# Softmax weights and q in one PSUM bank, output banks seeded by ScalarE, a half chunk in two matmuls, gate sums on GpSimd and ScalarE

## The chip, the core and the metric

The kernel runs on one core of a Trainium2 chip. The metric is the device time of one execution in microseconds, less being better. Engines are named as the profile names them: PE is TensorE (PEld its weight loads), DVE is VectorE, ACT is ScalarE, POOL is GpSimd, and SP is the queue that issues most transfers.

## The reference

For x of 2048 tokens by 640, a sliding, dilated attention (32 heads of 20, a window of 8 tokens at distance 2) is mixed by a gate per token with an MLP (640 to 1728 to 640, Mish):

```python
qkv = (x @ wqkv).reshape(B, S, 3, H, Dh)              # H = 32, Dh = 20
idx = pos[:, None] - 2 * arange(8)[None, :]           # idx < 0 is masked
logits = where(mask, einsum("bhsd,bhswd->bhsw", q, kg) * Dh ** -0.5, -1e9)
a = einsum("bhsw,bhswd->bhsd", softmax(logits), vg).reshape(B, S, D) @ wo
h = einsum("bsd,df->bsf", x, w1) + b1
b = einsum("bsf,fd->bsd", h * tanh(softplus(h)), w2)
g = sigmoid((x * gate_w).sum(-1, keepdims=True))
return g * a + (1 - g) * b
```

All data is float32.

## The kernel before

Every matrix product is made from split numbers: an operand X is kept as a high half (X rounded to fp32r, written by ScalarE) and a low half (X minus the high half, written by VectorE or GpSimd), both in one `pair` buffer, and `mm3` runs three matmuls: high by high, high by low, low by high. A matmul has up to 512 columns and adds into one PSUM bank of 128 x 512 floats.

The stages, in the order of TensorE's work: `qkv` makes q, k and v in eight units u (four groups of eight heads, two halves P of the tokens), each of eight banks with 496 columns; ScalarE empties these banks (`qkv_evac`). Between the units runs `mlp1`, the first MLP product, one bank of 15 matmuls per row chunk and token block, whose results (Mish on ScalarE) are stored, and partly summed with accumulating transfers issued by GpSimd (`plus`). Then `mlp2`, the second MLP product: it uses a scheme with seven block products (a, b, c, e, g, d, f in this order; `PRODUCTS`) in place of eight, over seven chunks kc of 128 rows; the seventh chunk of the second half of the 1728 rows has 64 real rows, and the rest is filled. Results of one product in a bank are copied out, and later products add on in the same bank, or VectorE adds the parts. Last, `wo_out` multiplies the attention's output by wo for each of four token blocks tb, and VectorE adds the gated MLP rows (L954) into the buffer that is sent out.

The attention itself (`attention`) runs on VectorE beside TensorE's work, in half units of four slots: `scores` multiplies q with a window of k (L424) and sums over the head's 20 elements (L427), `bounded` adds the mask to the first token's row on GpSimd (L435), `softmax` and `shares` make weights (L452, into `pw`), and `outputs` multiplies them with a window of v (L458) and adds up the window (L463 to L466). `turned_out` stores the result to `o`. `gate_dots` makes the gate sums on VectorE (L582).

The order of the work on each engine is set once, at build time, by `Plan.run`: a planner plays all tasks through with an estimated duration each, and gives every engine the ready task with the lowest rank. A task of engine "ANY" (most low halves) goes to GpSimd when one may run there, and to VectorE when it is due: its first matmul is less than NEAR nanoseconds of TensorE work away. While large attention tasks are left, GpSimd may start such tasks only in the stretches named quiet. Buffers come from rings (`bank`, `pair`, `raw`, `hb`, `w`), and a task that takes one waits for it.

Of the kernel before, what the change touches and what calls it, by code (L numbers as in the profile page):

```python
# [58 lines left out]
class Plan:  # L59


    NEAR, PATIENCE = 8000, 2000
# [31 lines left out]
    def run(self):  # L94
# [6 lines left out]
        loud = sum(t.kind != "" for t in self.tasks)  # L101
# [16 lines left out]
        def due(t):  # L118
            return now - t.rdy > self.PATIENCE if t.need is None else t.need - begun_pe < self.NEAR
# [9 lines left out]
        while left:  # L129
            again = not events or events[0][0] > now  # L130
            while again:
                again = False
                for e in self.LAG:
# [26 lines left out]
                    if e == "POOL" and on and quiet > now and gate and ins:  # L160
                        self.follow(ins, gate)
                    if e == "DVE":
                        if t.kind:
# [21 lines left out]
            if what == "idle":  # L185
                busy[x] = False
                continue
# [25 lines left out]
def kernel(ctx: ExitStack, tc: tile.TileContext, x, wq, wo, w1, b1, w2, xt, gw, out):  # L213
# [6 lines left out]
    psum = ctx.enter_context(tc.tile_pool(name="psum", bufs=8, space=PSUM))  # L220
# [8 lines left out]
    plan = Plan({"bank": 8, "pair": NPAIR, "w": NW, "raw": NRAW, "raw1": 1, "hb": NH,  # L229
                 "ot": 1, "b": 11}, follow)  # L230

    def ps_buf():
        return plan.buf("bank", lambda: psum.tile([128, 512], F32, name="bank"))
# [46 lines left out]
    bound = keep.tile([1, 7, 7], F32)  # L280
# [24 lines left out]
    pw = at.tile([128, 8, W, HQ], F32, name="pw")  # L305
# [18 lines left out]
    def consts_g():  # L324
        for i in range(2):
            G.memset(KV[i][0:1, 0:7], 0.0)

        G.memset(bound, 0.0)
        G.affine_select(bound, bound, pattern=[[1, 7], [1, 7]], compare_op=OP.is_ge,
                        fill=-BIG / scale, base=-7, channel_multiplier=0)  # L330
# [68 lines left out]
    freed = {}  # L399
    spilled = {}  # L400
# [3 lines left out]
    def attention(u, P, hq, ready, gates):  # L404
# [17 lines left out]
        def scores(s0, rank, after):  # L422
            def mul():
                return V.tensor_tensor(pr, window(kv, s0, 0), q[:, s0:s0 + 2, None, :].to_broadcast([128, 2, W, QF]), op=OP.mult)  # L424

            def red():
                V.tensor_reduce(lg_w[:, s0:s0 + 2], pr.rearrange("p s w (h d) -> p s w h d", d=DH), op=OP.add, axis=AX.X)  # L427

            step = chain(rank)
            step("DVE", 2850, mul, ready[s0] + after, kind="qk")  # L430
            return step("DVE", 2750, red, kind="qk sum")

        def bounded(a, b, after):
            b = min(b, 7)
            return add("POOL", 3400, lambda: G.tensor_tensor(lg[0:1, a:b, :, 0:7], lg[0:1, a:b, :, 0:7],  # L435
                       bound[:, a:b, None, :].to_broadcast([1, b - a, HQ, 7]), op=OP.add), [cg] + after, rank=-1)
# [9 lines left out]
        def shares(a, rank, after):  # L446
# [4 lines left out]
            step("DVE", 230, lambda: V.tensor_tensor(sm[:, h], sm[:, h], gate[:, P, h, None].to_broadcast([128, 4, HQ]), op=OP.mult), gates)  # L451
            return step("DVE", 650, lambda: V.tensor_tensor(pw[:, h].rearrange("p s w h -> p s h w"), lg[:, h], sm[:, h, :, None].to_broadcast([128, 4, HQ, W]), op=OP.mult))  # L452

        def outputs(s0, rank, after):
            def mul():
                vw = window(kv, s0, 1)
                vw = bass.AP(tensor=vw.tensor, offset=vw.offset, ap=[list(d) for d in vw.ap[:3]] + [[DH, HQ], [1, DH]])
                V.tensor_tensor(pr.rearrange("p s w (h d) -> p s w h d", d=DH), vw,  # L458
                                pw[:, s0:s0 + 2, :, :, None].to_broadcast([128, 2, W, HQ, DH]), op=OP.mult)

            step = chain(rank)
            step("DVE", 2850, mul, after, kind="pv")
# [15 lines left out]
        for i, a in enumerate((4, 0)):  # L478
            h = 2 * u + i
            read, used = shared_out.get(h - 2, (None, None))  # L480
            t1 = scores(a + 2, turn_of(h - 1, 0), [read, prev])
            t2 = scores(a, turn_of(h - 1, 3), [t1])
            e = softmax(a, turn_of(h - 1, 6), [bounded(a, a + 4, [t1, t2])])
            w = shares(a, turn_of(h, 1), [e, used])
# [588 lines left out]
```

## Time and profile before

| | |
|---|---|
| time, median of 3 runs | 639.48 us (639.43 to 639.97) |
| profiled execution | span 636.9 us from first to last instruction; the page gives no other time for it |
| TensorE | 631.9 us busy, 2805 matmuls, granted clock 1.00 |
| VectorE | 584.1 us busy, 584 instructions |
| ScalarE | 277.4 us busy, 565 instructions |
| GpSimd | 215.2 us busy, 157 instructions |
| transfers | 137 MB, 216 GB/s in the mean |

A row of the profile names the line of the kernel, the engine, the operation, the buffer written and those read, the count, the busy time and mean duration in ns of one instruction, and after the second bar the idle time ahead of them with what ended it. A row of the timeline begins with its start and its duration in us. Line numbers of before and of the changed kernel differ: in the changed one `mm3` is L410 to L412, the splits are L375 and L378, and the output copies are L1063.

### The profile page before, as it was taken

The numbers are of one execution on the slowest core, as the hardware profiler recorded it, in microseconds if no ns is written. First come the engines' busy times: TensorE is split into PE (matmuls) and PEld (weight loads), VectorE is DVE, ScalarE is ACT, GpSimd is POOL, SyncE is SP. The second block draws the span as 40 slices with busy tenths as digits, with TensorE's granted clock in tenths as the row PEclk, the third lists the DMA queues.
The fourth block names the chain that finished last, engine by engine and source line by source line (L and its number), as shares of the span: only waits on it lengthen the run. The fifth ranks groups of instructions, "written<-read, shape, count | busy, mean of one in ns | idle before, by whom it ended". The sixth has DMA issues, their size and how long they took to land.

```text
span 636.9 us, 8494 instructions
## 1 busy us (share of the span) xinstructions
PE 631.9 (99%) x2805; PEld 526.2 (83%) x2805; DVE 584.1 (92%) x584; ACT 277.4 (44%) x565; POOL 215.2 (34%) x157
## 2 busy tenths in 40 slices
PE   9999999999999999999999999999999999999997
PEld 6888888888888888888888888888888888888886
DVE  7888999999999999999899989799999999999941
ACT  7553353435436332542524244584676426721100
POOL 2212313131414442132343423204107328967310
PEclk9999999999999999999999999999999999999999
DMA  9999998867954994798499955989996758844642
GB/s 327 373 283 180 190 263 227 229 174 223 296 172 86 271 258 93 222 218 178 84 245 214 219 122 147 254 274 282 312 286 220 226 159 288 289 155 149 193 158 82
DMA packets 91323, 137.26 MB, mean 216 GB/s; under 512 B 12128, under 2 KB 41184, under 8 KB 91216
## 3 DMA queue, kind: packets, MB, share of 16 engines
q1 hardware_dynamic: 83600, 122.83, 62.6%
q0 software_dynamic: 7680, 13.90, 14.8%
q8 instruction: 22, 0.36, 0.2%
q14 instruction: 21, 0.17, 0.1%
HBM read 77.11 MB, written 57.81 MB: 212 GB/s over the span
## 4 chain that ended last, share of the span: by engine, by line
PE 99%; DVE 0%; issue 0%
PE bank L374 33%; PE bank L372 33%; PE bank L373 33%; PE bank L510 1%; PE bank L319 1%; DVE kvq L954 0%; DVE lg L315 0%
## 5 line engine op out<-in xcount | busy, mean ns | idle before, releaser
L372 PE MATMUL bank<-pair 128*128 128x512 f32 (+1 forms) x476 | 183.8, 386 | 0.0
L374 PE MATMUL bank<-pair 128*128 128x512 f32 (+1 forms) x476 | 183.7, 386 | 0.0
L373 PE MATMUL bank<-pair 128*128 128x512 f32 (+1 forms) x476 | 183.7, 386 | 0.0
L373 PEld LDWEIGHTS bank<-pair 128*128 128x128 f32 x476 | 89.3, 188 | 17.2
L374 PEld LDWEIGHTS bank<-pair 128*128 128x128 f32 x476 | 89.4, 188 | 17.1
L372 PEld LDWEIGHTS bank<-pair 128*128 128x128 f32 x476 | 89.3, 188 | 17.0
L424 DVE TENSOR_TENSOR pr<-kvq 128x2560 f32<-128x2560 f32 x32 | 90.8, 2839 | 3.5 <-DMA kvq<-kvq 1.6
L337 ACT ACTIVATE pair<-raw 128x512 fp32r<-128x512 f32 (+3 forms) x122 | 72.0, 615 | 48.4 <-DMA raw<-o 21.5
L458 DVE TENSOR_TENSOR pr<-kvq,pw 128x2560 f32<-128x2560 f32 x32 | 91.1, 2848 | 0.9
L427 DVE TENSOR_REDUCE lg<-pr 128x128 f32<-128x2560 f32 x32 | 90.2, 2818 | 0.6
L516 ACT ACTIVATE kvq<-bank 128x320 f32<-128x320 f32 x64 | 28.3, 442 | 114.7 <-PE bank L374 114.7
L435 POOL TENSOR_TENSOR lg<-lg,bound 1x168 f32<-1x168 f32 (+1 forms) x16 | 68.8, 4303 | 20.4 <-DVE lg L427 18.7
L625 ACT ACTIVATE hb<-bank,bias 128x512 f32<-128x512 f32 x52 | 35.9, 690 | 90.7 <-PE bank L374 77.2
L374 PE MATMUL bank<-pair,kvq 128*128 128x512 f32 (+1 forms) x188 | 72.6, 386 | 0.0
L372 PE MATMUL bank<-pair,kvq 128*128 128x512 f32 (+1 forms) x188 | 72.6, 386 | 0.0
L373 PE MATMUL bank<-pair,kvq 128*128 128x512 f32 (+1 forms) x188 | 72.6, 386 | 0.0
L340 POOL TENSOR_TENSOR pair<-raw,pair 128x496 fp32r<-128x496 f32 (+2 forms) x31 | 42.6, 1386 | 86.4 <-ACT pair L337 30.0
L372 PE MATMUL bank<-pair,w 128*128 128x512 f32 x182 | 70.8, 389 | 0.0
L373 PE MATMUL bank<-pair,w 128*128 128x512 f32 x182 | 70.8, 389 | 0.0
L374 PE MATMUL bank<-pair,w 128*128 128x512 f32 x182 | 70.8, 389 | 0.0
L340 DVE TENSOR_TENSOR pair<-raw,pair 128x512 fp32r<-128x512 f32 (+1 forms) x91 | 63.9, 721 | 5.2 <-ACT pair L337 5.2
L337 ACT ACTIVATE pair<-hb 128x512 fp32r<-128x512 f32 (+3 forms) x63 | 38.8, 615 | 42.7 <-DMA hb<-o 16.0
(89 smaller groups left out, 873.9 us busy)
## 6 DMA issues: line engine op xcount, KB each, us to landing
actt<-hb SPq DMA_DIRECT2D x52, 256.0 KB, 4.6
act<-hb SPq DMA_DIRECT2D x38, 256.0 KB, 4.6
raw<-actt SPq DMA_DIRECT2D x32, 256.0 KB, 4.5
raw<-act SPq DMA_DIRECT2D x29, 256.0 KB, 4.0
actt<-hb POOLq DMA_DIRECT2D x26, 256.0 KB, 6.2
actt<-actt POOLq DMA_DIRECT2D x24, 256.0 KB, 5.4
hb<-actt SPq DMA_DIRECT2D x24, 256.0 KB, 4.5
kvq<-in_xt SPq DMA_DIRECT2D x16, 320.0 KB, 7.2
```

The lines of the kernel that those rows point to most:

```text
L319: nc.tensor.matmul(warm_bank.t, idle[:, :128], idle, start=True, stop=True)
L337: a = add("ACT", act_ns(n), lambda: A.activation(hi(), raw(), AF.Copy), after, rank=rank, take=take, hold=hold)
L340: return (V if e == "DVE" else G).tensor_tensor(lo(), raw(), hi().bitcast(F32), op=OP.subtract)
L372: nc.tensor.matmul(ps, ah, bh, start=first, stop=False, skip_group_check=more)
L373: nc.tensor.matmul(ps, ah, bl, start=False, stop=False, skip_group_check=more)
L374: nc.tensor.matmul(ps, al, bh, start=False, stop=last, skip_group_check=more)
L424: return V.tensor_tensor(pr, window(kv, s0, 0), q[:, s0:s0 + 2, None, :].to_broadcast([128, 2, W, QF]), op=OP.mult)
L427: V.tensor_reduce(lg_w[:, s0:s0 + 2], pr.rearrange("p s w (h d) -> p s w h d", d=DH), op=OP.add, axis=AX.X)
L435: return add("POOL", 3400, lambda: G.tensor_tensor(lg[0:1, a:b, :, 0:7], lg[0:1, a:b, :, 0:7], bound[:, a:b, None, :].to_broadcast([1, b - ...
L458: V.tensor_tensor(pr.rearrange("p s w (h d) -> p s w h d", d=DH), vw, pw[:, s0:s0 + 2, :, :, None].to_broadcast([128, 2, W, HQ, DH]), op=O ...
L516: a = add("ACT", 330, lambda: A.activation(kv[:, 7 + s], ps.t[:, QF:3 * QF].rearrange("p (a b) -> p a b", a=2), AF.Copy), [done] + before, ...
L625: a = add("ACT", 595, lambda: A.activation(to(it()), src(), AF.Mish, bias=bias[:n, fc:fc + 1]), after + [bias_in], rank=NEXT, take=[] if h ...
```

## The change

1. One of eight banks, `side`, holds the softmax weights of two slots (`pw`) and a copy of two slots of q (`qs`), which ScalarE writes ahead of each score product. So both large attention products read one operand from PSUM. Seven banks are left for matmuls. The planner keeps ScalarE's copies of q apart from VectorE's instructions that touch this bank, and lets GpSimd start work beside all three kinds of large attention instructions.
2. ScalarE writes ("seeds") banks with values that TensorE then adds onto: the products c and d start from a bank that holds the earlier sum, and the output banks from the gated MLP rows. ScalarE copies the output banks out (L1063). For token blocks 2 and 3 the output is made in two parts, of three chunks and of two.
3. In products b, g and f the last chunk is loaded twice, into both halves of the partitions, as high and low numbers of the same 64 rows, and two matmuls take the place of three (`load_low_w`, `load_low_act`).
4. The gate sums are a product on GpSimd and a sum on ScalarE. The mask's bound is written by small ScalarE instructions instead of added on GpSimd.
5. NEAR is 5000 plus 2000 for each waiting task that is needed earlier, and VectorE takes tasks that are not due when it has nothing else.

```diff
-    NEAR, PATIENCE = 8000, 2000
+    NEAR, TURN, PATIENCE = 5000, 2000, 2000
...
         def due(t):
-            return now - t.rdy > self.PATIENCE if t.need is None else t.need - begun_pe < self.NEAR
+            if t.need is None:
+                return now - t.rdy > self.PATIENCE
+            ahead = sum(x.need is not None and x.need < t.need for x in shared)
+            return t.need - begun_pe < self.NEAR + self.TURN * ahead
...
-                        fit += [t for t in shared if fits(t) and (not on or due(t))]
+                        any_ = [t for t in shared if fits(t)]
+                        fit += [t for t in any_ if not on or due(t)]
+                        if inside["ACT"] == "qs":
+                            fit = [t for t in fit if t.kind not in TOUCH]
+                        fit = fit or any_
+                    elif e == "ACT" and inside["DVE"] in TOUCH:
+                        fit = [t for t in fit if t.kind != "qs"]
...
-                        if t.kind == "qk sum":
                             quiet, gate = now + t.ns, last
+                        if t.kind in TOUCH:
+                            if copied:
+                                self.follow(ins, copied)
+                            touched, copied = ins, None
...
-    psum = ctx.enter_context(tc.tile_pool(name="psum", bufs=8, space=PSUM))
+    NBANK = 7
+    psum = ctx.enter_context(tc.tile_pool(name="psum", bufs=1, space=PSUM))
+    banks = [psum.tile([128, 512], F32, name=f"bank{i}") for i in range(NBANK)]
...
-    pw = at.tile([128, 8, W, HQ], F32, name="pw")
+    side = psum.tile([128, 512], F32, name="side")
+    pw = side[:, :2 * W * HQ].rearrange("p (s w h) -> p s w h", w=W, h=HQ)
+    qs = side[:, 2 * W * HQ:2 * W * HQ + 2 * QF].rearrange("p (s f) -> p s f", f=QF)
...
         def bounded(a, b, after):
             b = min(b, 7)
-            return add("POOL", 3400, lambda: G.tensor_tensor(lg[0:1, a:b, :, 0:7], lg[0:1, a:b, :, 0:7],
-                       bound[:, a:b, None, :].to_broadcast([1, b - a, HQ, 7]), op=OP.add), [cg] + after, rank=-1)
+            def run():
+                for s in range(a, b):
+                    A.activation(lg[0:1, s, :, 0:7 - s], bound[:, :, 0:7 - s], AF.Copy)
+            return add("ACT", 220 * (b - a), run, [cg] + after, rank=-1)
...
-            done.append(add("DVE", 750, lambda i=i, s=s: V.tensor_tensor_reduce(
-                at(i), at(i), at(0), op0=OP.mult, op1=OP.add, scale=1.0, scalar=0.0, accum_out=zt[:, P, s:s + 1]), [g] + gw_in, rank=NEXT))
+            t = add("POOL", 1750, lambda i=i: G.tensor_tensor(at(i), at(i), at(0), op=OP.mult), [g] + gw_in, rank=NEXT)
+            done.append(add("ACT", 800, lambda i=i, s=s: A.activation(at(i), at(i), AF.Copy, accum_out=zt[:, P, s:s + 1]), [t], rank=NEXT))
...
+    def twice(raw, src, n, after=()):
+        def both():
+            for a in (0, FR):
+                nc.sync.dma_start(raw.t[a:a + FR, :n], src())
+        return [add("SP", 900, both, after, take=[raw], size=n * 512)]
+
+    def load_low_w(src, n, sign, after=()):
+        raw, p = stage(True), pair_buf()
+        d = twice(raw, src, n, after)
+        a = add("ACT", act_ns(n), lambda: A.activation(p.t[:, 0, :n], raw.t[:, :n], AF.Copy, scale=sign), d, rank=SOON, take=[p], hold=[raw])
+        b = add("DVE", dve_ns(n), lambda: V.scalar_tensor_tensor(p.t[FR:, 0, :n], raw.t[FR:, :n], sign, p.t[FR:, 0, :n].bitcast(F32),
+                op0=OP.mult, op1=OP.subtract), [a], rank=SOON, hold=[raw, p])
+        c = add("ACT", act_ns(n), lambda: A.activation(p.t[:FR, 1, :n], raw.t[:FR, :n], AF.Copy, scale=sign), [a], rank=SOON, hold=[raw, p])
+        z = add("POOL", 320, lambda: G.memset(p.t[FR:, 1, :n].bitcast(F32), 0.0), [a], rank=-0.3, hold=[p])
...
+        def seed(key, z, after):
+            bank[key] = ps_buf(seeded=True)
+            seeds[key] = copy(bank[key], z, after, [bank[key]])
...
+                            if low:
+                                nc.tensor.matmul(bank[key].t, p.t[:, 0, c:c + 128], acts[P].t[:, 0], start=False, stop=False, skip_group_check=more)
+                                nc.tensor.matmul(bank[key].t, p.t[:, 1, c:c + 128], acts[P].t[:, 1], start=False, stop=True, skip_group_check=more)
+                                continue
...
+        if seeded:
+            t, take = add("ACT", 590, lambda: A.activation(by_slot(ps.t), as_slots(b.t), AF.Copy), b.ready, rank=SOON, take=[ps], hold=[b]), []
...
+        if last:
+            v = add("ACT", 590, lambda: A.activation(as_slots(b.t), by_slot(ps.t), AF.Copy), [t], rank=SOON, hold=[ps, b])
+            dma(lambda: out[tb, dc], lambda: b.t, [v], rank=0.0, hold=[b])
+        else:
+            v = add("DVE", 690, lambda: V.tensor_tensor(as_slots(b.t), by_slot(ps.t), as_slots(b.t), op=OP.add),
+                    [t] + b.ready, rank=SOON, hold=[ps, b])
```

How the built order moves, at three places. First TensorE, at the end of product f and the first matmul of the output, before (`pair` buffers with their numbers; `kvq0` then holds wo):

```order
L372 MATMUL bank_4696<-pair_4966,pair_4931 128x512
L373 MATMUL bank_4696<-pair_4966,pair_4931 128x512
L374 MATMUL bank_4696<-pair_4966,pair_4931 128x512
L372 MATMUL bank_4696<-pair_4984,pair_4969 128x512
L373 MATMUL bank_4696<-pair_4984,pair_4969 128x512
L374 MATMUL bank_4696<-pair_4984,pair_4969 128x512
L372 MATMUL bank_5101<-pair_4989,kvq0_4452 128x512
```

The same place on TensorE after the change:

```order
L410 MATMUL bank3_66<-pair_4966,pair_4940 128x512
L411 MATMUL bank3_66<-pair_4966,pair_4940 128x512
L412 MATMUL bank3_66<-pair_4966,pair_4940 128x512
L988 MATMUL bank3_66<-pair_4994,pair_4977 128x512
L989 MATMUL bank3_66<-pair_4994,pair_4977 128x512
L410 MATMUL bank5_68<-pair_5002,kvq0_4206 128x512
```

The last chunk has two matmuls per bank in place of three, and the output's first matmul comes onto bank 5, which ScalarE has written.

Second ScalarE, before, from the last loads of f into the first token block of the output: only splits (L337) and one exponential (L444).

```order
L337 ACTIVATE pair_5001<-hb_4939 128x512
L337 ACTIVATE pair_5008<-raw_4951 128x512
L337 ACTIVATE pair_5020<-raw_4971 128x512
L337 ACTIVATE pair_5032<-hb_4982 128x512
L444 ACTIVATE lg_215<-lg_215 128x256
```

After the change, ScalarE at that place (L1056 seeds an output bank, L887 copies a bank of f out):

```order
L375 ACTIVATE pair_5044<-hb_4981 128x512
L1056 ACTIVATE bank5_68<-raw_4975 128x4x4x32
L1056 ACTIVATE bank6_69<-hb_4986 128x4x4x32
L375 ACTIVATE pair_5066<-raw_5000 128x512
L887 ACTIVATE kvq1_220<-bank0_63 128x512
L375 ACTIVATE pair_5075<-hb_5005 128x512
L887 ACTIVATE kvq1_220<-bank4_67 128x512
L375 ACTIVATE pair_5087<-raw_5019 128x512
L887 ACTIVATE kvq1_220<-bank2_65 128x512
L1056 ACTIVATE bank1_64<-kvq1_220 128x4x4x32
```

Seeds and copies of banks now stand between the splits; the seed of bank 1 needs the copy of bank 0 and a product with the gate on GpSimd.

Third the end of the kernel. Before, VectorE added the last banks:

```order
L954 TENSOR_TENSOR raw_5350<-bank_5487,raw_5350 128x512
L954 TENSOR_TENSOR kvq1_213<-bank_5505,kvq1_213 128x512
L954 TENSOR_TENSOR kvq1_213<-bank_5523,kvq1_213 128x512
L954 TENSOR_TENSOR kvq1_213<-bank_5541,kvq1_213 128x512
L1067 UNCONDITIONAL_BRANCH
```

After the change the last rows are ScalarE's:

```order
L1063 ACTIVATE kvq1_220<-bank6_69 128x512
L1056 ACTIVATE bank5_68<-kvq1_220 128x4x4x32
L1063 ACTIVATE kvq1_220<-bank1_64 128x512
L1056 ACTIVATE bank6_69<-kvq1_220 128x4x4x32
L1063 ACTIVATE hb_5153<-bank0_63 128x512
L1063 ACTIVATE raw_5236<-bank4_67 128x512
L1063 ACTIVATE raw_5242<-bank2_65 128x512
L1063 ACTIVATE kvq1_220<-bank3_66 128x512
L1063 ACTIVATE kvq1_220<-bank5_68 128x512
L1063 ACTIVATE kvq1_220<-bank6_69 128x512
```

Six copies follow the last seed, and each copies one bank as TensorE finishes it.

More of the change, by code (lines that the diff above doesn't have):

```diff
@@ L838, in after_product @@
                         z = y[key] = zp[key]
-                        z.done = two("DVE", z, z, bank["u", P, j], OP.add, [ends["c", "u", P, j], z.done])
+                        z.done = copy(z, bank["u", P, j], [ends["c", "u", P, j]])
                     elif name == "e":
@@ L865, in mlp2 @@
             kcs = [kc, kc + 1] if kc in (0, KH - 2) else [kc]
+            if name == "d" and kc == 0:
+                for P in range(2):
+                    for j in range(2):
+                        seed(("v", P, j), y[P, j], [y[P, j].done])
             while ahead < min(len(steps), i + len(kcs) + 3):
```

205 lines of the change are left out of this document (133 added, 72 removed).

## Prediction

> **What bounds the kernel now.** I read the page's top first, then the chain of waits, then TensorE's waits, then stretches of 50 us.
>
> ```profile
> span 636.9 us, 8494 instructions
> PE 631.9 (99%) x2805; PEld 526.2 (83%) x2805; DVE 584.1 (92%) x584; ACT 277.4 (44%) x565; POOL 215.2 (34%) x157
> PE 99%; DVE 0%; issue 0%
> PEld bank L510 <- ACT pair L337: 0.5, 1, 0.5
> ```
>
> The chain is TensorE from end to end, and the only wait of a real matmul on another engine is the first one's, 0.5 us. A busy TensorE is not yet a TensorE without gaps, because matmul ends are modelled, so I looked at starts. The timeline's matmuls of L374 near the end, the first and the last of a run:
>
> ```profile
> 615.06 0.39 PE L374 MATMUL bank<-pair,kvq 128*128 128x512 f32 x1
> 632.74 0.39 PE L374 MATMUL bank<-pair,kvq 128*128 128x512 f32 x1
> 633.17 0.69 DVE L954 TENSOR_TENSOR kvq<-bank,kvq 128x512 f32<-128x512 f32 x1 [2.71 <-PE bank L374]
> ```
>
> Between the first two lie 78 matmuls: 17.68 / 78 = 0.2267 us from start to start. In the timeline of the whole span no two neighbouring matmuls after 10.5 us start more than 0.24 us apart. So the time before is a count of matmuls times their pace, a head of about 5 us, and a tail: last start 632.74, the addition from 633.17 to 633.86, and 3.0 us for the last output transfer, to 636.9. The median of 639.48 is 2.6 us above this span; I carry that difference over unchanged.
>
> How far TensorE was from waiting shows in the stretches (columns: TensorE, weight loads, VectorE, ScalarE, GpSimd busy, with counts):
>
> ```profile
> 450.00:500.00 50.00, 50.00 (x222) 41.38 (x222) 49.83 (x64) 31.91 (x58) 15.45 (x5) 1.00 0.85 272
> 550.00:600.00 50.00, 50.00 (x222) 41.41 (x221) 49.73 (x54) 13.88 (x25) 36.04 (x17) 1.00 0.56 182
> 582.57 1.77 DVE L340 TENSOR_TENSOR pair<-hb,pair 128x512 fp32r<-128x512 f32 x1
> 584.69 0.39 PE L372 MATMUL bank<-pair,kvq 128*128 128x512 f32 x1
> ```
>
> VectorE is as full as TensorE there. The last two rows are the tightest place: the low half that ends at 584.34 belongs to the pair that the matmul at 584.69 reads first (by the order). It was 0.35 us early. Before holds no stall, but little room.
>
> **The half chunk.** In products b, g and f the last chunk has 64 real rows. Its three matmuls per bank become two (L988, L989): 6 + 6 + 4 banks, 16 matmuls of 512 columns less, 2789 against 2805. At 0.2267 us that is 3.63 us, all on the path. Nothing hides behind them, since no gap stands between matmuls. The nine 64-row loads are each issued twice by SP (load_low_w, load_low_act); against that six fills of the upper 64 rows fall away, so SP has three issues more, at about 0.4 us each by the first row below (two in 0.79), and a transfer lands in 4.5 us by the second, while three steps are loaded ahead: hidden. If that cover went, one late load would cost at most its landing time, 4.5 us.
>
> ```profile
> 561.91 0.79 SPq L346 DMA_DIRECT2D raw<-b  x2
> raw<-actt SPq DMA_DIRECT2D x32, 256.0 KB, 4.5
> ```
>
> **Seeds.** ScalarE writes 28 banks (4 u, 4 v, 20 of the output) before TensorE adds onto them, and takes over the 20 output copies. No row shows a seed. The nearest copies:
>
> ```profile
> L804 ACT ACTIVATE kvq<-bank 128x512 f32<-128x512 f32 x16 | 9.3, 589 | 3.3 <-PE bank L374 3.3
> L821 POOL TENSOR_TENSOR kvq<-kvq,w 128x512 f32<-128x512 f32 x5 | 12.4, 2484 | 0.0
> L337 ACT ACTIVATE pair<-raw 128x512 fp32r<-128x512 f32 (+3 forms) x122 | 72.0, 615 | 48.4 <-DMA raw<-o 21.5 <-DMA raw<-act 9.0 <-DMA raw<-actt 6.4
> ```
>
> On the path a seed costs between 0 (written while TensorE works on another bank) and 0.6 us plus a handover (all 28 late: 17 us). I take 0, by the tightest place that the order shows, the step from f to the output. The first output group's third bank is gated from f's first bank: f ends that bank 45 matmuls, 10.2 us, before its seed is needed. Between stand nine instructions of ScalarE (5.4 us) and, partly beside them, one product on GpSimd (2.5 us): 7.9 us at most. The first two output banks are seeded from rows spilled long before. In the last part (two chunks, 6 matmuls, 1.36 us a bank) six of ten seeds precede the part; the other four and ten copies are 14 x 0.6 = 8.4 us in 13.6 us.
>
> **Seven banks.** One bank now holds q and the weights. Before, ScalarE emptied a bank within one instruction of its last matmul and waited for TensorE:
>
> ```profile
> L516 ACT ACTIVATE kvq<-bank 128x320 f32<-128x320 f32 x64 | 28.3, 442 | 114.7 <-PE bank L374 114.7
> L520 ACT ACTIVATE hx<-bank 128x16 f32<-128x16 f32 x64 | 12.7, 198 | 0.0
> L337 ACT ACTIVATE w<-raw 128x640 fp32r<-128x640 f32 x13 | 9.6, 737 | 4.8 <-DMA raw<-in_w 4.8
> ```
>
> 114.7 us of idle time ahead of those copies mean that banks are free early. A bank is 15 matmuls (3.3 us), so ScalarE may be almost 20 us late before six others are used up. Cost 0. The 32 copies of q (0.44 us each by the first row), 56 small writes for the bound (0.2 by the second) and 16 sums (0.74 by the third), with the seeds and copies above, lift ScalarE from 277 to about 350 us, 55% of the span. Each q copy and each bound waits for VectorE, and splits for TensorE queue behind; idle ScalarE time covers that.
>
> **VectorE and GpSimd.** The groups that go, shrink or grow:
>
> ```profile
> L582 DVE CUSTOM_DVE_ANT_0 kvq<-kvq 128x640 f32<-128x640 f32 x16 | 13.6, 904 | 0.3 <-DMA kvq<-in_xt 0.3
> L340 DVE TENSOR_TENSOR pair<-raw,pair 128x512 fp32r<-128x512 f32 (+1 forms) x91 | 63.9, 721 | 5.2 <-ACT pair L337 5.2
> L954 DVE TENSOR_TENSOR kvq<-bank,kvq 128x512 f32<-128x512 f32 x10 | 6.7, 682 | 9.4 <-PE bank L374 9.4
> L435 POOL TENSOR_TENSOR lg<-lg,bound 1x168 f32<-1x168 f32 (+1 forms) x16 | 68.8, 4303 | 20.4 <-DVE lg L427 18.7
> L452 DVE TENSOR_TENSOR pw<-lg,sm 128x256 f32<-128x256 f32 x16 | 11.6, 723 | 0.5
> L808 DVE TENSOR_TENSOR kvq<-kvq,bank 128x512 f32<-128x512 f32 x8 | 5.3, 672 | 0.0
> L821 DVE TENSOR_TENSOR kvq<-kvq,w 128x512 f32<-128x512 f32 x5 | 3.3, 678 | 0.0
> L458 DVE TENSOR_TENSOR pr<-kvq,pw 128x2560 f32<-128x2560 f32 x32 | 91.1, 2848 | 0.9
> L340 POOL TENSOR_TENSOR kvq<-raw,kvq 128x640 fp32r<-128x640 f32 x4 | 6.7, 1670 | 10.0 <-ACT kvq L337 10.0
> L340 POOL TENSOR_TENSOR pair<-raw,pair 128x496 fp32r<-128x496 f32 (+2 forms) x31 | 42.6, 1386 | 86.4 <-ACT pair L337 30.0 <-DVE pr L424 29.7 <-DVE pair L340 10.3
> ```
>
> VectorE loses the 16 sums (15 us with their reads), 43 low halves (43 x 0.72 = 31), 14 sums of products (9.5) and ten output additions (6.8), 62 us in all. It gains some 6 us: smaller weight products, 32 at about 0.4 instead of 16 at 0.72, five more signed halves, three more gate products. About 528 us, 83%. The 64 large products with an operand in a bank keep their 2.8 us (bounds 2.7 and 2.9): the L954 and L808 instructions with a bank operand take 0.67 to 0.68, as the gate products of L821 without one do. GpSimd loses 69 us and gains 16 products (1.7 each, 27 us) and 38 low halves (1.4 each, 53 us): about 225 us. None of this is on the path, so its worth is 0 us; what it buys is room in the two stretches above. NEAR falls from 8 to 5 us plus 2 us for each earlier task, which takes some room back.
>
> What GpSimd costs VectorE shows in these rows:
>
> ```profile
> 198.12 0.82 DVE L464 TENSOR_TENSOR pr<-pr 128x640 f32<-128x640 f32 x1
> 361.24 2.15 POOL L340 TENSOR_TENSOR pair<-raw,pair 128x512 fp32r<-128x512 f32 x1
> 362.28 1.80 DVE L464 TENSOR_TENSOR pr<-pr 128x640 f32<-128x640 f32 x1
> 363.91 0.68 POOL L435 TENSOR_TENSOR lg<-lg,bound 1x224 f32<-1x224 f32 x1
> 530.79 25.72 POOL L435 TENSOR_TENSOR lg<-lg,bound 1x224 f32<-1x224 f32 x1 [0.47 <-DVE lg L427]
> 563.56 1.74 POOL L340 TENSOR_TENSOR pair<-raw,pair 128x512 fp32r<-128x512 f32 x1
> 564.07 0.68 DVE L808 TENSOR_TENSOR kvq<-kvq,bank 128x512 f32<-128x512 f32 x1
> 570.52 6.37 POOL L821 TENSOR_TENSOR kvq<-kvq,w 128x512 f32<-128x512 f32 x2
> ```
>
> Beside a GpSimd subtraction the pure-SBUF L464 took 1.80 us (0.82 alone), while L808, one operand in a bank, kept 0.68. The Trainium skill, "SBUF — State Buffer", section "Who interferes with whom", says the same: a VectorE instruction with two SBUF inputs contends with GpSimd's reads, one with at most one does not. By that rule the large products may run beside GpSimd at no cost; the trace agrees for L808 only.
>
> **Tail and head.** The last copy is ScalarE's, 0.59 us for VectorE's 0.69: -0.1 us, bounds -0.1 to +0.2. The first twelve VectorE instructions keep their order: 0.
>
> **Sum.** 636.9 - 3.63 - 0.1 = 633.2 us of span, and 2.6 around it: 635.8 us. Runs before differ by 0.5 us, so this case alone gives 635.3 to 636.4.
>
> **Rivals.**
>
> 1. *Small stalls.* NEAR's shorter lead or a late GpSimd half lets TensorE wait in a few places of the second MLP product. For: 0.35 us of room at 584 us, and nearly twice the low halves on GpSimd. Against: 56 us less VectorE work. Three to eight waits of 0.5 us: 1.5 to 4 us, so 637.3 to 639.8. The part up to 638.2 is still faster, the rest no change.
> 2. *A starved GpSimd product (slower).* The bound's addition above took 25.72 us in a stretch where VectorE ran mostly pure-SBUF instructions, and 0.68 us elsewhere. If a low half that TensorE reads is caught so after the attention, when nothing keeps GpSimd apart from VectorE, TensorE stands. It decides from a wait of 3.7 + 1.3 = 5 us in all, beyond the half's lead; a 128x512 product held 10 us with 3 us of lead gives 7 us: 643 us. Against: the slowest 128x512 work in before is two in 6.37 us. A long stand may also slow what follows, since the first nine matmuls (L319), after a still TensorE, start 0.43 us apart: 9 x 0.2 = 1.8 us more.
>
> ```profile
> 2.03 0.15 PEld L319 LDWEIGHTS <-lg 128*128 128x128 bf16 x1 [0.28 <-issue]
> 2.46 0.15 PEld L319 LDWEIGHTS <-lg 128*128 128x128 bf16 x1 [0.28 <-issue]
> ```
>
> The Trainium skill, "TensorE: Matmul & The Clock Gate", section "What's actually happening", halves the clock after about 3.4 us without work; by that rule the 1.8 us are due after such a stand, and the granted clock of 1.00 in every stretch here shows no such case.
> 3. *The edits cost the path directly.* Every seed late by its handover: 28 x 0.1 = 2.8 us, 638.6, no change. Against: the order gives each seed several banks of lead.
>
> **Numbers.** 0.2% (1.3 us) is about what a measurement of this kernel can tell from none. No stall: 0.66, 635.8 us. Rival 1: 0.20, of it 0.13 below 638.2. Rival 3: 0.04. Rival 2: 0.10. So faster 0.66 + 0.13 = 0.79, same 0.07 + 0.04 = 0.11, slower 0.10. The range 635.2 to 638.5 leaves out rival 2, part of 1 and 3 and a little below, about 0.19.
>
> **What would show it.** Right: 2789 matmuls, TensorE the whole chain, starts never over 0.24 us apart, VectorE near 83%, GpSimd's L435 group gone, large VectorE products at 2.8 us beside GpSimd, span near 633.2. Wrong: PEld rows with idle time released by ScalarE (a seed) or GpSimd (a low half), a GpSimd product of several us ahead of such a row, or large VectorE products longer than 2.9 us.

## The result, and the profile after

The changed kernel takes 642.61 us (median of 5, 641.70 to 645.47) against 639.48 for the kernel before, a ratio of 1.0058 (95%: 1.0039 to 1.0078): slower, where 635.8 us and faster were predicted. It also varies by almost 4 us from run to run; the kernel before varies by 1.

The page of the changed kernel, its engines and its chain; then the waits of TensorE's weight loads (total us, times, longest):

```profile
span 639.8 us, 8572 instructions
PE 630.4 (99%) x2789; PEld 523.8 (82%) x2789; DVE 539.3 (84%) x503; ACT 334.5 (52%) x744; POOL 222.8 (35%) x200
PE 92%; DMA 2%; DVE 2%; POOL 1%; issue 1%; SPq 0%; ACT 0%; DVEq 0%; POOLq 0%; ACTq 0%
PEld bank L411 <- DVE pair L378: 5.0, 2, 3.9
```

The loads of the engines are close to those predicted, and the 2789 matmuls are as predicted. But the chain is no longer TensorE from end to end, and 5.0 us of waits for VectorE's low halves are new, in two places. Both lie in product f. A wait of TensorE between two matmuls is called a stand or a gap below; its length is given from the start of the matmul ahead of it to the start of the one behind it, where 0.23 us is the normal step. TensorE's timeline there:

```profile
551.32 0.39 PE L410 MATMUL bank<-pair 128*128 128x512 f32 x1
552.45 0.50 PE L411 MATMUL bank<-pair 128*128 128x512 f32 x1 [0.74 <-DVE pair L378]
552.78 0.40 PE L412 MATMUL bank<-pair 128*128 128x512 f32 x1
...
553.71 0.39 PE L410 MATMUL bank<-pair 128*128 128x512 f32 x1
557.53 0.56 PE L411 MATMUL bank<-pair 128*128 128x512 f32 x1 [3.43 <-DVE pair L378]
557.88 0.63 PE L412 MATMUL bank<-pair 128*128 128x512 f32 x1
558.31 0.63 PE L410 MATMUL bank<-pair 128*128 128x512 f32 x1
...
560.87 0.57 PE L410 MATMUL bank<-pair 128*128 128x512 f32 x1
561.28 0.39 PE L411 MATMUL bank<-pair 128*128 128x512 f32 x1
```

From 551.32 to 552.78 pass 1.46 us for two steps, 1.0 us too much; from 553.71 to 557.53 pass 3.82 for one, 3.6 too much; then nine steps to 561.28 take 3.75 us, 1.7 too much (the granted clock was 0.55 from 557.5 to 561.3 us and 1.00 ahead of it and behind it). Sum 6.3 us. The span before, to two places, is 636.86: 636.86 - 3.63 + 6.31 = 639.54. The tail from the last start (635.42) to the end is 4.40 us for 4.12 before, 0.28 more, which gives the span of 639.82. No other two starts behind the head lie more than 0.24 us apart.

What VectorE and GpSimd did meanwhile (after the last large attention product, L501, which ended at 535.6):

```profile
541.39 1.77 DVE L891 TENSOR_TENSOR kvq<-hb,kvq 128x512 f32<-128x512 f32 x1
543.09 2.57 DVE L511 TENSOR_TENSOR pr<-pr 128x1280 f32<-128x1280 f32 x1
545.69 1.80 DVE L512 TENSOR_TENSOR pr<-pr 128x640 f32<-128x640 f32 x1
...
551.49 0.91 DVE L378 TENSOR_TENSOR pair<-hb,pair 128x512 fp32r<-128x512 f32 x1
552.31 3.45 DVE L908 TENSOR_TENSOR kvq<-kvq,w 128x512 f32<-128x512 f32 x2
555.69 1.79 DVE L378 TENSOR_TENSOR pair<-raw,pair 128x512 fp32r<-128x512 f32 x1
```
```profile
540.87 3.44 POOL L891 TENSOR_TENSOR kvq<-raw,kvq 128x512 f32<-128x512 f32 x2
544.27 7.57 POOL L908 TENSOR_TENSOR kvq<-kvq,w 128x512 f32<-128x512 f32 x4
551.79 1.75 POOL L378 TENSOR_TENSOR pair<-hb,pair 128x512 fp32r<-128x512 f32 x1
```

The two L378 of VectorE are the low halves that TensorE stood for; they end at 552.40 and 557.48. Almost every VectorE instruction with two inputs in SBUF takes some 1.0 to 1.1 us longer than without GpSimd beside it (1.77 for 0.68, 1.80 for 0.81, 2.57 for 1.48), and the GpSimd instructions are slowed too (1.55 to 2.54 for 1.29). L908 are the gate products of d's results, the work of lowest rank in the program: six of them run in this stretch, on both engines at once. In the kernel before, the same stretch of product d and f looked like this on VectorE:

```profile
543.13 0.68 DVE L808 TENSOR_TENSOR kvq<-kvq,raw 128x512 f32<-128x512 f32 x1
543.73 0.68 DVE L340 TENSOR_TENSOR pair<-raw,pair 128x512 fp32r<-128x512 f32 x1
...
558.84 0.68 DVE L340 TENSOR_TENSOR pair<-hb,pair 128x512 fp32r<-128x512 f32 x1
```

GpSimd held one 1x224 addition (L435) from 530.79 to 556.51, and VectorE ran its 128x512 instructions at 0.68 us each. The number of instructions did not grow: from 535 to 560.5 us VectorE started 41 instructions and GpSimd one; in the changed kernel they started 20 and 12.

One run of an experiment below had a granted clock of 0.75 throughout, and one of the kernel before took 2618.6 us; both are left out of the times.

### The profile page after: what moved, and what is told of

It is laid out like the page before. It is cut to its first block, busy times and chain, and to the rows that moved or that the text cites. A ratio compares the mean times of both kernels' runs of the same rounds, so it can differ in the third digit from the quotient of the medians.

```text
span 639.8 us, 8572 instructions
## 1 busy us (share of the span) xinstructions
PE 630.4 (99%) x2789; PEld 523.8 (82%) x2789; DVE 539.3 (84%) x503; ACT 334.5 (52%) x744; POOL 222.8 (35%) x200
## 4 chain that ended last, share of the span: by engine, by line
PE 92%; DMA 2%; DVE 2%; POOL 1%; issue 1%; SPq 0%; ACT 0%; DVEq 0%; POOLq 0%; ACTq 0%
PE bank L411 30%; PE bank L412 30%; PE bank L410 30%; DVE pair L378 1%; PE bank L557 1%; DMA raw<-actt 1%; DMA raw<-o 1%; PE bank L359 1%; DMA hb<-actt 1%; POOL pair L378 1%; DMA b<-raw 1%; POOL kvq L891 0%; PE bank L989 0%; PE bank L988 0%; POOL kvq L908 0%
## 5 line engine op out<-in xcount | busy, mean ns | idle before, releaser
L411 PE MATMUL bank<-pair 128*128 128x512 f32 (+1 forms) x460 | 178.3, 388 | 4.2 <-DVE pair L378 4.2
L412 PE MATMUL bank<-pair 128*128 128x512 f32 (+1 forms) x460 | 178.2, 387 | 0.0
L410 PE MATMUL bank<-pair 128*128 128x512 f32 (+1 forms) x460 | 178.2, 387 | 0.0
L378 POOL TENSOR_TENSOR pair<-raw,pair 128x512 fp32r<-128x512 f32 (+2 forms) x51 | 67.4, 1338 | 144.6 <-ACT pair L375 48.7
L411 PEld LDWEIGHTS bank<-pair 128*128 128x128 f32 x460 | 86.8, 189 | 21.7 <-DVE pair L378 5.0
L410 PEld LDWEIGHTS bank<-pair 128*128 128x128 f32 x460 | 86.8, 189 | 16.7
L412 PEld LDWEIGHTS bank<-pair 128*128 128x128 f32 x460 | 86.6, 188 | 16.5
L463 DVE TENSOR_TENSOR pr<-kvq,side 128x2560 f32<-128x2560 f32 x32 | 90.2, 2817 | 11.6 <-ACT side L469 11.2
L501 DVE TENSOR_TENSOR pr<-kvq,side 128x2560 f32<-128x2560 f32 x32 | 90.3, 2820 | 1.1
L375 ACT ACTIVATE pair<-raw 128x512 fp32r<-128x512 f32 (+2 forms) x113 | 66.3, 612 | 28.6 <-DMA raw<-o 12.1
L411 PE MATMUL bank<-pair,kvq 128*128 128x512 f32 (+1 forms) x188 | 72.6, 386 | 0.0
L411 PE MATMUL bank<-pair,w 128*128 128x512 f32 x182 | 70.8, 389 | 0.0
L378 DVE TENSOR_TENSOR pair<-raw,pair 128x512 fp32r<-128x512 f32 (+3 forms) x62 | 48.0, 791 | 19.4 <-ACT pair L375 19.4
L660 POOL DMA_DIRECT2D actt<-actt x28 | 25.6, 958 | 87.7 <-DMA actt<-actt 25.3
L511 DVE TENSOR_TENSOR pr<-pr 128x1280 f32<-128x1280 f32 x32 | 50.6, 1582 | 0.9
```

The source lines that it names most:

```text
L375: a = add("ACT", act_ns(n), lambda: A.activation(hi(), raw(), AF.Copy), after, rank=rank, take=take, hold=hold)
L378: return (V if e == "DVE" else G).tensor_tensor(lo(), raw(), hi().bitcast(F32), op=OP.subtract)
L410: nc.tensor.matmul(ps, ah, bh, start=first, stop=False, skip_group_check=more)
L411: nc.tensor.matmul(ps, ah, bl, start=False, stop=False, skip_group_check=more)
L412: nc.tensor.matmul(ps, al, bh, start=False, stop=last, skip_group_check=more)
L463: return V.tensor_tensor(pr, window(kv, s0, 0), qs[:, :, None, :].to_broadcast([128, 2, W, QF]), op=OP.mult)
```

## The experiments

The times (before in the same sessions: 639.1 us):

| kernel | median us (lowest to highest) | ratio to before, 95% |
|---|---|---|
| before + half chunk alone | 637.65 (635.88 to 641.16) | 0.9966 to 0.9997 |
| changed, gate products held | 636.23 (635.77 to 637.21) | 0.9947 to 0.9971 |
| changed, subtractions on VectorE | 640.19 (636.98 to 644.68) | 1.0002 to 1.0038 |
| changed, gate products on GpSimd | 640.35 (639.62 to 641.76) | 1.0015 to 1.0033 |
| changed, both edits | 635.94 (635.24 to 636.28) | 0.9933 to 0.9960 |
| changed, without half chunk | 645.74 (644.81 to 648.66) | 1.0093 to 1.0129 |
| changed, old NEAR | 640.70 (639.83 to 644.24) | 1.0019 to 1.0050 |
| changed, GpSimd kept apart through f | 635.79 (635.54 to 636.66) | 0.9937 to 0.9965 |
| the same, second session | 636.02 (635.10 to 643.61) | 0.9940 to 0.9991 |
| both edits, `side` in SBUF | 661.80 (659.71 to 664.69) | 1.0334 to 1.0392 |

**The half chunk alone**, put into the kernel before (`load_low_w`, `load_low_act`, two matmuls; f's weights keep their sign there).

> The kernel before with the half chunk alone (point 3 of the change); banks, attention, gate sums, seeds and the planner's rules as before. If a removed matmul is worth its pace and the stand in product f comes from the other points: 16 x 0.2267 = 3.6 us off, 635.8 us, no two matmul starts after the head over 0.3 us apart. If the doubled loads and the extra small instructions of the half chunk make the stand: a gap of 2 us or more in product f, 638 to 641 us.

The fastest run, 635.88 us, is the sum of the prediction (639.48 - 3.63 = 635.85); the median keeps 1.5 us of the 3.6. The profiled run took 640.52 us. TensorE, VectorE and GpSimd in it:

```profile
579.16 0.39 PE L372 MATMUL bank<-pair,kvq 128*128 128x512 f32 x1
581.04 0.50 PE L373 MATMUL bank<-pair,kvq 128*128 128x512 f32 x1 [1.50 <-DVE pair L340]
...
582.74 0.51 PE L373 MATMUL bank<-pair,kvq 128*128 128x512 f32 x1 [0.73 <-DVE pair L340]
...
583.98 0.63 PE L374 MATMUL bank<-pair,kvq 128*128 128x512 f32 x1
584.41 0.63 PE L372 MATMUL bank<-pair,kvq 128*128 128x512 f32 x1
...
576.49 2.82 DVE L458 TENSOR_TENSOR pr<-kvq,pw 128x2560 f32<-128x2560 f32 x1
579.23 0.68 DVE L992 TENSOR_TENSOR kvq<-bank,kvq 128x512 f32<-128x512 f32 x1
579.83 1.16 DVE L340 TENSOR_TENSOR pair<-raw,pair 128x512 fp32r<-128x512 f32 x1
...
578.33 2.11 POOL L340 TENSOR_TENSOR pair<-raw,pair 128x512 fp32r<-128x512 f32 x1 [8.86 <-ACT pair L337]
```

There are two stands, of 1.9 and 1.1 us, and nine matmuls at 0.43 us behind them. They lie in the output bank in which the kernel before had 0.35 us to spare (at 584 us), though at its first two pairs and not at its last. TensorE comes to this bank 2.8 us sooner (579.16 for 581.97), and VectorE makes the two halves only after a large attention product (576.49 to 579.31), with GpSimd beside it. Neither theory has it right: the matmuls are worth their pace, but the stand is not in f, and no row points at the half chunk's own work. That the faster TensorE has eaten the lead of its producers is a reading of these rows; no run here tests it.

**Who makes the stand in f.** Three edits of the changed kernel, in one session: the gate products of d's results wait for the end of f; the subtractions L891 only on VectorE; the same gate products only on GpSimd.

The edit of the first (`spilled` leaves out the rows that went through memory):

```diff
-            return [add("ANY", either("ANY", 512), run, after + [gb_in[tb // 2]], rank=LAST, hold=[b, gbs[tb // 2]])]
+            held = [] if b.spilled or tb % 2 == 0 else [ends["f", "v", 1, 1]]
+            return [add("ANY", either("ANY", 512), run, after + held + [gb_in[tb // 2]], rank=LAST, hold=[b, gbs[tb // 2]])]
...
+                buf.spilled = True
```

> The changed kernel with the six gate products of product d's results held back until TensorE has ended product f. Theory 1 (these gate products, on GpSimd beside VectorE and on VectorE ahead of two of f's low halves, make the stand): the 1.1 and 3.8 us gaps and the slow matmuls behind them go, 635.8 to 636.5 us, and nothing new late, since the rows are wanted some 17 us after f. Theory 2 (f's loads come late because GpSimd's two subtractions of d's results release staging buffers late): the gap shrinks by at most half, 638 to 641 us. Theory 3 (the planner's shorter lead): no change, 641 to 644 us.

> The changed kernel with the four subtractions of product d's results all on VectorE (two were on GpSimd); the gate products stay free to go to either. Theory 2: the staging buffers come free 2 us or more earlier, the low halves of f are early, 635.8 to 637 us. Theory 1: GpSimd starts its gate products earlier but still runs them beside VectorE's sums and low halves, some gap of 1 us or more remains, 638 to 643 us.

> The changed kernel with the same six gate products pinned to GpSimd, so none stands ahead of a low half in VectorE's row, while GpSimd works longer beside VectorE. If the order in VectorE's row is the larger part (3.45 us of the 3.8): the second gap shrinks to about 0.3 us and the slow matmuls behind it go, 636.5 to 638 us. If contention alone is the larger part: low halves on VectorE stay at 1.7 to 1.8 us each while GpSimd multiplies, gaps of 2 us or more remain, 639 to 643 us.

Holding the gate products takes away 6.4 us, and no wait stands in f: theory 1. In the profiled run the only wait for a half is one of 0.9 us for GpSimd at 455 us (`PEld bank L411 <- POOL pair L378: 0.9, 1, 0.9`). GpSimd still makes halves beside VectorE's there, and VectorE's still take long:

```profile
553.97 1.82 DVE L378 TENSOR_TENSOR pair<-hb,pair 128x512 fp32r<-128x512 f32 x1
```

None is late, so the longer instructions alone do not make the stand. With only the subtractions moved, a gap of 2.8 us and slow matmuls stay, and the time wanders from 637 to 645: the late release of staging buffers (theory 2) is part of it at most. With no gate product ahead of a half in VectorE's row, the second gap shrinks from 3.8 to 1.0 us and the slow matmuls go, so the order makes much of the stand's length. But gaps of 1.1 and 1.0 us stay, both released by VectorE's halves beside a busy GpSimd, and behind f there is a new one of 1.8 us, where the first output seed waited for a gate product that VectorE made late (L908, ScalarE idle 4.1 us for it). The time is still 640.4 us, but not for f alone: of some 6 us that the profiled run (641.8 us) took beyond the predicted 635.8, about 2.3 lie in f, 1.5 at that seed, and 2.0 at 74 us, where TensorE stood for a bank (see "Seven banks" below).

**Both edits together.**

> The changed kernel with both edits of the runs before: the gate products of d's results held until product f has ended, and the four subtractions on VectorE. If what is left over after holding the gate products (636.2 us, 0.4 over the sum of the prediction) is chance in the transfers: 635.8 to 636.5 us. If the subtractions on GpSimd still cost a little in f: 0.3 us less than with the gate products held alone. If VectorE misses GpSimd's help there: 636.5 to 638 us and a gap in f.

635.94 us, 0.3 us below the gate products alone, inside the scatter of both. It beats the kernel before by 0.53% (0.40 to 0.67%) and comes to the 635.8 that was predicted, with another order of work than the one the prediction was made for.

**Two other suspects: TensorE's earlier arrival, and the planner's lead.** The changed kernel without the half chunk, and with `NEAR, TURN = 8000, 0`.

> The changed kernel without the half chunk (2805 matmuls, three per bank in the last chunk again; the 64 fill rows are written again). Theory E (the stand comes because TensorE reaches f's first pairs earlier, by 12 of the 16 matmuls, 2.7 us, while VectorE and GpSimd are not earlier): the low halves that were 1.1 and 3.8 us late are early or at most 1 us late, no slow matmuls, 639.4 to 640.5 us, so the half chunk in the changed kernel brings no gain or a loss (642.6 with it). Theory N (the stand is made by the gate products whatever TensorE does): it stays at 5 us or more with its slow matmuls, 644 to 646 us.

> The changed kernel with the planner's old lead (NEAR 8000, no TURN). It moves many low halves between VectorE and GpSimd in the whole second MLP product. Theory 3 (the shorter lead makes the stand): 635.8 to 637 us. Theory 1: after the attention the rule does not apply any more, the gate products still go to both engines at the start of f, a gap of over 2 us stays, 638 to 645 us.

Without the half chunk the time is 645.74 us, so theory E falls as an account of the time: in the changed kernel too the half chunk gains 3.1 us of its 3.6, and it is the rest of the change that costs 6.7 us (645.74 against 639.08). In the profiled run TensorE stood five times for VectorE's halves (7.3 us), two of them in f (1.9 and 2.1 us), and none was followed by slow matmuls; once more it stood 2.3 us for a bank, at 75 us. The loss in f is smaller than with the half chunk, some 3.8 us for 6.3, which is what an earlier TensorE would add there, so theory N does not hold as written either. But this is one profiled run, at 648.7 us the slowest of its five. With the old lead, 640.7 us: theory 3 falls, since at most 1.9 us of the loss go, and the intervals overlap. Its profiled run had gaps of 1.3 us at 471 us (GpSimd's half), of 1.9 us in f (VectorE's half) and of 1.0 us behind it (a seed).

**Contention or amount of work.** GpSimd is kept apart until TensorE starts the last task of f. VectorE does everything itself, with six gate products standing between f's halves. One of the lines of the edit (`calm` counts the tasks of f that are not yet started):

```diff
-                    on = begun and loud
+                    on = begun and (loud or calm)
```

> The changed kernel with GpSimd kept apart from VectorE until TensorE starts the last task of product f (the planner's rule lasted only while large attention instructions were left). VectorE then makes all four subtractions, all of f's low halves and all six gate products itself, the gate products standing between f's low halves, and GpSimd does nothing beside it. Theory C (contention: it is GpSimd's company that makes VectorE's work late, not its amount): VectorE's instructions of 128x512 take 0.68 us, not 1.78, no gap over 1 us in f, 635.8 to 637 us. Theory A (amount and order: 14 more instructions on VectorE, gate products ahead of halves): low halves are later than in the changed kernel, gaps of several us, 643 us or more.

> The same kernel as the one with GpSimd kept apart until product f, for a profile at full clock (the profiled run before had a granted clock of 0.75 throughout). By theory C: 635.5 to 636.7 us, VectorE's 128x512 instructions between the last large attention product and the end of f at 0.68 us, and no two matmul starts over 0.3 us apart in f. By theory A the 635.8 us came in spite of late low halves somewhere, and gaps of 0.5 us or more stand in f.

635.79 and 636.02 us. VectorE in the second one's profile:

```profile
546.72 0.68 DVE L908 TENSOR_TENSOR kvq<-kvq,w 128x512 f32<-128x512 f32 x1
547.33 0.69 DVE L378 TENSOR_TENSOR pair<-raw,pair 128x512 fp32r<-128x512 f32 x1
...
548.76 0.69 DVE L908 TENSOR_TENSOR kvq<-kvq,w 128x512 f32<-128x512 f32 x1
549.37 0.69 DVE L378 TENSOR_TENSOR pair<-hb,pair 128x512 fp32r<-128x512 f32 x1
...
560.89 1.79 DVE L378 TENSOR_TENSOR pair<-raw,pair 128x512 fp32r<-128x512 f32 x1
```

With 13 more instructions on VectorE (516 for 503) and gate products ahead of halves, nothing is late, and no two starts in f lie more than 0.24 us apart: each instruction takes 0.68 us until GpSimd starts again at 560.58, and from the next one on 1.8. That is theory C. A gate product ahead of a half costs so much because it takes 1.75 us in place of the 0.6 from start to start; the amount of work is not the cause. The stand needs both, work of low rank ahead of the halves and GpSimd beside it: without the first (gate products held) or without the second (here) it is gone. GpSimd's help in this stretch was worth less than nothing. One of ten runs of the second session took 643.6 us; why is open.

**The PSUM operand.** In the kernel with both edits only the place of `side` is changed; the order on each engine is the same.

```diff
-    side = psum.tile([128, 512], F32, name="side")
+    side = at.tile([128, 512], F32, name="side")
```

> The kernel with both edits (gate products held, subtractions on VectorE; 635.9 us), in which only the place of the tile with the softmax weights and q is changed: SBUF in place of the PSUM bank. The order on every engine is the same, instruction for instruction. If an operand in PSUM keeps VectorE's large products clear of GpSimd: the products of L463 and L501 beside GpSimd take 3.5 to 4 us in place of 2.8, GpSimd's products beside them 2 to 4 us in place of 1.3, low halves come late, 645 to 680 us. If the place of the operand makes no difference: 636 us and 2.8 us.

26 us slower. Groups of the kernel with both edits, then of this one:

```profile
L501 DVE TENSOR_TENSOR pr<-kvq,side 128x2560 f32<-128x2560 f32 x32 | 90.2, 2820 | 1.1
L511 DVE TENSOR_TENSOR pr<-pr 128x1280 f32<-128x1280 f32 x32 | 49.5, 1547 | 0.9
L378 POOL TENSOR_TENSOR pair<-raw,pair 128x512 fp32r<-128x512 f32 (+2 forms) x51 | 65.2, 1294 | 146.5 <-ACT pair L375 46.7 <-PE bank L412 28.8 <-DVE lg L487 20.6
```
```profile
L501 DVE TENSOR_TENSOR pr<-kvq,side 128x2560 f32<-128x2560 f32 x32 | 92.1, 2878 | 1.1
L511 DVE TENSOR_TENSOR pr<-pr 128x1280 f32<-128x1280 f32 x32 | 60.2, 1883 | 0.9
L378 POOL TENSOR_TENSOR pair<-raw,pair 128x512 fp32r<-128x512 f32 (+2 forms) x51 | 118.4, 2334 | 105.6 <-ACT pair L375 59.8 <-DMA raw<-in_wo 14.1 <-DVE lg L487 7.8
```

The total was foretold, the way only in part: the large products hardly lengthen in the mean (four of 64 took 3.4 to 4.2 us). It is GpSimd's halves that are drawn out, from 1.29 to 2.33 us in the mean and to 3.9 us at most, and the small sums behind the large products (1.55 to 1.88). TensorE's longest wait, 4.5 us, is for a half made by GpSimd.

**What a stand costs TensorE after it.** Chosen stands, made by k small ScalarE copies between two matmuls of one bank (in all 682.8 and 659.2 us).

> The changed kernel with the gate products held, and eight chosen stands of TensorE inside banks of the first MLP product, made by k small ScalarE copies (96 columns, some 0.26 us each, between the rows of 16 and 320 columns) that wait for a matmul and that the next one waits for: k = 4, 8, 14, 6, 11, 18, two of 5 with two thirds of a bank between them, and 2. It does extra work, nothing is left out. Rule of the prediction (one stand of 3.4 us or more slows what follows): only k = 14 and 18 (3.7 and 4.7 us), with 8 to 9 matmuls at 0.43 us after each, about 1.7 us a time. Rule by share (about 2.5 us of standing within some 4 us, as in the runs with 1.9 + 1.1 and with 2.8 us): k = 11, 14, 18 and perhaps the pair of 5, while k = 8 and less cost their own length alone.

> The changed kernel with the gate products held, and eight single stands of TensorE, made by k = 5, 6, 7, 5, 6, 7, 5, 6 small ScalarE copies (about 2.0, 2.3 and 2.6 us from start to start). It does extra work, nothing is left out. If a length decides (no slow matmuls after 1.7 to 2.3 us, slow ones after 2.33 and longer, in the runs so far): none of the k = 5 is followed by matmuls at 0.43 us, both k = 7 are. If it depends on where the stand falls in time: stands of equal length differ.

From start to start the stands were 1.07, 1.70, 2.02 (four times), 2.08, 2.33 (four times), 2.65 (twice), 2.96, 3.90, 4.85 and 6.10 us. Up to 2.08 none was followed by a group of matmuls at 0.43 us; of those at 2.33 two were and two were not; from 2.65 on all were, 7 to 13 of them. The pair of 2.0 us each, 4 us apart, was not. The first of these two kernels has a stand that was not chosen, for a seed, of 2.33 us too, and ten slow matmuls follow it. Stands of 2.24 and 2.31 us for a bank, in the experiments above, were not followed by any. Two stands of 2.33 us in the second kernel:

```profile
102.69 0.39 PE L413 MATMUL bank<-kvq,w 128*128 128x512 f32 x1
105.03 0.71 PE L411 MATMUL bank<-kvq,w 128*128 128x512 f32 x1 [1.94 <-ACT gap L420]
105.53 0.63 PE L412 MATMUL bank<-kvq,w 128*128 128x512 f32 x1
...
216.42 0.39 PE L413 MATMUL bank<-pair,w 128*128 128x512 f32 x1
218.75 0.50 PE L411 MATMUL bank<-pair,w 128*128 128x512 f32 x1 [1.94 <-ACT gap L420]
219.09 0.39 PE L412 MATMUL bank<-pair,w 128*128 128x512 f32 x1
```

So neither rule holds as written: for a single stand the length that decides is about 2.3 us, not 3.4, and at that length equal stands end differently. Nor is it the longest single stand alone: in the kernel before with the half chunk, 1.9 and 1.1 us with 0.6 us of matmuls between them were followed by nine.

## Why the prediction was wrong

- **The half chunk**: right in its count and its price, 2789 matmuls and 3.6 us. All of it is kept only where no new stand eats it: the two best versions reach 635.8 and 635.9, and the half chunk alone reaches 635.9 in its fastest run, but its median keeps 1.5 us.
- **VectorE and GpSimd**: the step that failed is "None of this is on the path, so its worth is 0 us; what it buys is room". The loads were about right (539, 223 and 335 us for 528, 225 and 350), the conclusion was not. The planner keeps GpSimd apart only while large attention products are left. Their last one, before and after:

```profile
578.12 2.83 DVE L458 TENSOR_TENSOR pr<-kvq,pw 128x2560 f32<-128x2560 f32 x1
532.74 2.82 DVE L501 TENSOR_TENSOR pr<-kvq,side 128x2560 f32<-128x2560 f32 x1
```

  In the changed kernel it starts 45 us sooner, now ahead of f, and so the rule ends sooner too. The room was at once filled with gate products, which the kernel before began at 559.44 on VectorE and at 569.00 on GpSimd, and with subtractions on GpSimd (L891), where before VectorE did the sums of this stretch (L808) alone. They put GpSimd beside VectorE's two-SBUF-input work for some 13 us, just where f's first halves are due. Two runs show it: hold the gate products (-6.4 us), or keep GpSimd away (-6.8). With all of them on GpSimd, the halves that are still late (1.1 and 1.0 us) stand beside it too. The prediction had the price of it in a row, 1.80 us for 0.82, and asked only whether the large products would pay it; its signs of being wrong named waits for ScalarE and GpSimd, and none for VectorE. That GpSimd's long L435 addition, which the change took away, had kept this stretch quiet before is seen in the profile, but no run puts it back.
- **Rival 2** was nearest: it named the moment "after the attention, when nothing keeps GpSimd apart from VectorE" and gave 643 us for the 642.6 measured. Its victim was wrong. Not GpSimd's half was caught, but VectorE's, and its chance of 0.10 rested on looking for a starved GpSimd product alone. That its number fits is luck: it stands for one GpSimd product held for 10 us, and no GpSimd product in f took over 2.6 us.
- **Slow matmuls after a stand**: nine of them, 1.7 us for the 1.8 of rival 2.
- **Rival 1**, small stalls: the old lead gives 640.7, at most 1.9 us better and no clear difference. A late GpSimd half, its other ground, is seen at 455 us in the kernels with the gate products held (waits of 0.9 and 0.6 us).
- **Seeds**: 0, right in the changed kernel, where no matmul waited for a seed. Matmuls waited for one (1.4 and 0.6 us in the profiled runs) in the kernels with the gate products on GpSimd and with the old lead; they also did with `side` in SBUF (1.2) and in the first kernel with chosen stands (1.95).
- **Seven banks**: "ScalarE may be almost 20 us late" is too much. In the profiled runs of three experiments (gate products on GpSimd, no half chunk, `side` in SBUF) TensorE stood at 72 to 75 us for a bank that ScalarE had yet to empty (`L567`). Without the half chunk, ScalarE had waited 7.2 us for a buffer whose store was issued at 53.5 us and took 11.4 us. In the kernel with both edits the same wait was 2.3 us: the store took 10.1 us there, but was issued 4 us sooner.

```profile
PEld bank L410 <- ACT hx L567: 2.3, 1, 2.3
64.92 0.69 ACT L672 ACTIVATE hb<-bank,bias 128x512 f32<-128x512 f32 x1 [7.20 <-DMA actt<-hb]
```

  ScalarE emptied that bank 5.2 us later than in the kernel with both edits and TensorE lost 2.1 us, so the lead there, by an estimate from these two numbers, is about 3 us. The term of 0 was too small in these runs by up to 2.1 us. The stand is not in the changed kernel's profile, and how much of its scatter comes from it was not measured.
- **Tail**: +0.3 us for -0.1, a little over the upper bound of +0.2.

## What to carry to other kernels

Work taken off an engine that is not the bound is not free of effect: ask which waiting work will take the room, on which engines at once, and what becomes due beside it. A low-rank instruction that slows work on a deadline is best held until the deadline is past, or done by the same engine; here that is worth 6.4 us of 642.6. And when a consumer gets faster, read the smallest lead of each producer: where it is smaller than the gain, part of the gain may go again, as in most runs of the half chunk alone.

## What the runs showed of the hardware

- VectorE's 128x512 instructions with both inputs in SBUF took 0.68 us alone and mostly 1.75 to 1.80 beside a GpSimd product; GpSimd's took 1.29 alone and 1.5 to 2.5 beside them. With one input in a PSUM bank the 2.82 us of a large product did not change (2808 to 2823 ns over 32); with both in SBUF it took 2.88 in the mean, and GpSimd's halves 2.33 in place of 1.29. The Trainium skill, "SBUF — State Buffer", section "Who interferes with whom", states that a VectorE instruction with two SBUF inputs contends with GpSimd's reads and one with at most one, outside VectorE's two-port modes, does not; these runs agree.
- Stands from 2.65 us on were always followed by matmuls at half pace (0.43 us for 0.227), in groups of 7 to 13; of five stands of 2.33 us three were, and so were 1.9 and 1.1 us with 0.6 us between them. The Trainium skill, "TensorE: Matmul & The Clock Gate", section "What's actually happening", lets the clock fall after at least one idle window of about 3.4 us that runs free of the program. That equal stands differ agrees with a free-running window; the length does not agree, and the measured 2.3 us is what counts here.
